# Batch 1 of an attention and MLP kernel: the last weight quarter issued later, behind a square on GpSimd; state products moved ahead of scores; groups that read that quarter moved behind the values

## The chip, the core and the metric

The kernel runs on one core of a Trainium2 chip. The core has five engines that run side by side and wait for each other through semaphores: TensorE (matmuls; PE in the profile, its weight loads PEld), VectorE (DVE), ScalarE (ACT), GpSimd (POOL) and SyncE (SP), which here only issues DMAs. Each engine works its own instructions strictly in the order of the program. Sixteen DMA engines move data between HBM and the on-chip memory SBUF; DMAs are issued from the queues of SP (loads, stores, transposes) and of POOL (weight loads that cast from float32 to float16 on the way). Matmul results stand in PSUM, which has eight banks, and an engine has to read a bank before another result may take its place.

The metric is the device time of one execution in microseconds. Before the change the median of 3 runs is 296.44 us (296.11 to 296.5).

## What is computed

Retention (attention without a softmax, with a decay by distance) of 8 batches, 8 heads, 576 positions and head size 64, and behind it an MLP on all 4608 tokens whose activation is x + sin²(αx)/α:

```python
scores = (1/8) * q @ k.T                       # per batch and head
ret    = scores * D                            # D[i, j] = gamma_h**(i - j) for i >= j, else 0
x      = (ret @ v)                             # heads side by side: 4608 x 512
h      = x @ w_in                              # 512 -> 2048
g      = h + sin(alpha * h)**2 / (alpha + 1e-9)
out    = g @ w_out                             # 2048 -> 512
```

## The kernel before

**Attention of a batch.** The first 512 positions of a batch are taken in two pieces (p = 0, 1) of 256 positions, each in two chunks of 128. For each piece `load` brings q, k and v from HBM (512 KB each, on SP's queue), `cast` turns them into float16 with the decay factors multiplied in, and q and k are transposed (for batch 1 on TensorE by `turn`, with `take` copying the result out of PSUM). Inside a chunk the retention is computed directly: `scores` (16 small matmuls for a half of the heads of a piece), `masked` (a VectorE multiplication with the mask), `values`. What lies in earlier chunks comes in through a state: `outer((p,))` computes the state products k-transposed times v of piece p (32 small matmuls of 64x64), `take_sum` copies them out, `more` adds the earlier chunks' sum (GpSimd), `to_state` makes the float16 state of it, and `add_states` multiplies it with q. `keep` copies the finished x of a piece out of PSUM. `values(p, True)`, which adds the second part, and `add_states` follow `values(p, False)`.

**MLP of a block** of 512 tokens. For each of 16 slices of the inner dimension (u or fc = 0 to 15) `project` multiplies x with w_in (4 matmuls of 512 columns), `sine` is ScalarE's sine, `square` its square (on ScalarE, VectorE or GpSimd, by the last argument A_, V or G_), and `product` on VectorE makes the slice of g, called gT, and with that releases the projection's bank. The second multiplication is done in groups: `gemm2(0, u, bank)` with u = 4c + part multiplies the 128 tokens of quarter c with the slices 4·part to 4·part + 3 of w_out, 4 matmuls of 512 columns, into the bank of quarter c; after the four parts `finish(0, c)` copies the bank out (ScalarE) and stores it (SP). So the groups 3, 7, 11 and 15 read the last quarter of w_out, which `load_w_out(3)` loads (one DMA on POOL's queue, a cast from float32 on the way).

**Order.** Everything up to batch 4 is written out by hand, instruction by instruction; each engine's order is the order of these lines. The code around the change finishes the MLP of block 0 while it does the attention of batch 1 and then begins the MLP of block 1 (`project(1, 7, ...)`, which needs both `keep` of batch 1). The buffers of the float32 loads (`raw0` to `raw5`) and of the squares (`ss0` to `ss3`) are reused in a fixed order, and banks are named by hand ("op", "h0" to "h2" single, "m0", "m1" double).

The steps of which the prediction speaks:

- L908 to L919: square 10 on GpSimd, the state of batch 0 (`to_state(3, G_)`), and the issue of the last quarter of w_out, all on POOL; L937 to L938, the load and GpSimd cast of the first v piece ("v0") of batch 1; L949 to L950 the same for its second k piece ("k1"); L957 to L958 the load of its second v piece ("v1") and its cast on ScalarE.
- L945 to L972: on TensorE the scores of piece 0, the state products of piece 0, groups 5 and 6, the transposition of k1, group 14, the scores of piece 1, group 15, the state products of piece 1 (`outer((1,), ...)`, which need the cast of v1), groups 7 and 0.
- L974 to L1013: the values and added states of both pieces, groups 1 and 2, and the two `keep`; L978 is VectorE's cast of q of batch 2.
- L1014 to L1024: projections 7 and 6, group 3, sines 7 and 6, square 6, `finish(0, 0)`, projection 13 into bank "h2", projection 8 into "op".

In the profile all projections bear the line L568, all groups L605, all casts of k and q L207, all copies on ScalarE L120, on VectorE or GpSimd L122; scores are L389, masks L401, state products L325, values L430, added states L451.

Of the kernel before, what the change touches and what calls it, by code (L numbers as in the profile page):

```python
# [36 lines left out]
def kernel(  # L37
# [68 lines left out]
    V, A_, G_ = nc.vector, nc.scalar, nc.gpsimd  # L106
# [5 lines left out]
    def load_w_out(g):  # L112
        nc.gpsimd.dma_start(w_out16[:, 4 * g : 4 * g + 4, :], w_out_r[:, g])
# [4 lines left out]
    def copy(eng, d_, s_):  # L118
        if eng is nc.scalar:
            eng.copy(d_, s_)  # L120
        else:
            eng.tensor_copy(d_, s_)  # L122
# [4 lines left out]
    def place(tag, shape, dtype):  # L127

        name = tag + next(slot_of[tag])
        if name not in places:  # L130
            places[name] = work.tile(shape, dtype, tag=name, bufs=1, name=name)
        return places[name]
# [14 lines left out]
    def load(b, nm, p):  # L147
        if p < 2 and b >= HALVED and nm != "q":
            t_ = place("raw", [P, H, 2 * D], F32)
            for g in range(2):  # L150
                for r in range(2):
                    s0 = 256 * p + 128 * g + 64 * r
                    nc.sync.dma_start(
                        t_[halves(g), :, r * D : r * D + D], src[nm][b, :, s0 : s0 + 64, :].rearrange("h i d -> i h d")
                    )
        elif p < 2:
            t_ = place("raw", [P, H, 2 * D], F32)
            nc.sync.dma_start(
                t_, src[nm][b, :, 256 * p : 256 * p + 256, :].rearrange("h (i r) d -> i h (r d)", r=2)
            )  # L160
        else:
            if b % 2 == 0:
                if b < 4:
                    raw[b, nm, 2] = work.tile([P, H, D], F32, tag="raws", bufs=3, name=nm + "s32")
                else:
                    raw[b, nm, 2] = ends_home(b, nm)
            t_ = raw[b - b % 2, nm, 2]
            nc.sync.dma_start(t_[halves(b % 2)], src[nm][b, :, 512:576, :].rearrange("h i d -> i h d"))
        raw[b, nm, p] = t_
# [77 lines left out]
    def take(b, nm, p, eng, ys=(0, 1)):  # L247
        d_ = new_T(b, nm, p).rearrange("p x n -> p (x n)")
        cols = slice(512 * ys[0], 512 * ys[-1] + 512)
        copy(eng, d_[:, cols], trs[b, nm, p][:, cols])  # L250
# [304 lines left out]
    def bank(tag):  # L555
        if tag[0] == "m":
            return psum.tile([P, 2, 512], F32, tag=tag, bufs=1, name="hps")[:, 0]
        return psum.tile([P, 512], F32, tag=tag, bufs=1, name="hps")

    def project(n, fc, tag, part=None):  # L560

        if n not in gT:
            gT[n] = work.tile([P, FC, 512], F16, tag="gT", bufs=2, name="gT")
        if (n, fc) not in hps_of:
            hps_of[n, fc] = [bank(tag), None]
        cols = PART[part]
        for a in range(KT):
            matmul(  # L568
                hps_of[n, fc][0][:, cols], w_in16[fc // 4][:, a, fc % 4 :: 4], xs[n][:, a, cols],
                start=(a == 0 and part != 1), stop=(a == KT - 1), skip_group_check=True,  # L570
            )

    def sine(n, fc):
        hps = hps_of[n, fc][0]
        s_t = place("s", [P, 512], F16)
        nc.scalar.activation(  # L576
            s_t, hps, mybir.ActivationFunctionType.Sin, bias=0.0, scale=alpha_t[:, fc : fc + 1],
        )
        hps_of[n, fc][1] = s_t

    def square(n, fc, eng):
        s_t = hps_of[n, fc][1]
        ss_t = place("ss", [P, 512], F16)
        if eng is nc.scalar:
            nc.scalar.activation(ss_t, s_t, mybir.ActivationFunctionType.Square)  # L585
        else:
            eng.tensor_tensor(ss_t, s_t, s_t, MULT)  # L587
        hps_of[n, fc][1] = ss_t

    def product(n, fc):  # L590
        hps, ss_t = hps_of.pop((n, fc))
        nc.vector.scalar_tensor_tensor(gT[n][:, fc, :], ss_t, inva[:, fc : fc + 1], hps, MULT, ADD)  # L592

    def finish(n, c, eng=None):
        osb = work.tile([P, 512], F32, tag="osb", bufs=4, name="osb")
        copy(eng or nc.scalar, osb, ops[n, c, 0])
        r0 = 576 * n + 128 * c
        nc.sync.dma_start(out[r0 : r0 + 128, :], osb)

    def gemm2(n, u, tag, cols=slice(0, 512)):  # L600
        c, part = divmod(u, 4)
        if (n, c, cols.start) not in ops:
            ops[n, c, cols.start] = psum.tile([P, 512], F32, tag=tag, bufs=1, name="ops")
        for fk in range(4 * part, 4 * part + 4):
            matmul(  # L605
                ops[n, c, cols.start][:, cols], gT[n][:, fk, c * P : (c + 1) * P], w_out16[:, fk, cols],
                start=(fk == 0), stop=(fk == FC - 1), skip_group_check=True,
            )
# [113 lines left out]
    at = [Attention(b) for b in range(B)]  # L722
# [13 lines left out]
    def wait_for_w_in(g):  # L736

        nc.sync.dma_start(gate, w_in16[g][:, 0, 0:64])
# [42 lines left out]
    with tc.manual_schedule():  # L781
# [134 lines left out]
        sine(0, 10)  # L916
        square(0, 10, G_)
        at[0].to_state(3, G_)
        load_w_out(3)  # L919
        wait_for_w_in(3)  # L920
        product(0, 5)
        project(0, 14, "h2")
# [3 lines left out]
        sine(0, 12)  # L926
        at[1].scores(0, 0, "m1")
        at[1].masked(0, 0)
        square(0, 12, A_)
        project(0, 13, "h0")  # L930
        sine(0, 13)
        square(0, 13, A_)
# [10 lines left out]
        product(0, 13)  # L943
        product(0, 12)
        at[1].scores(0, 1, "m0")  # L945
        at[1].outer((0,), "h0", "h1")
        at[1].take_sum(1, A_)
        gemm2(0, 5, "op")
        load(1, "k", 1)  # L949
        cast(1, "k", 1, G_)  # L950
        gemm2(0, 6, "op")
# [9 lines left out]
        take(1, "k", 1, V, (1,))  # L961
        take(1, "k", 1, V, (0,))
        gemm2(0, 14, "h2")
        at[1].scores(1, 1, "m0")
        at[1].masked(1, 1)
        at[1].scores(1, 0, "m1")
        at[1].masked(1, 0)
        gemm2(0, 15, "h2")
        at[1].outer((1,), "h0", "h1")
        at[1].take_sum(2, A_)  # L970
        at[1].more(2)
        gemm2(0, 7, "op")  # L972
        gemm2(0, 0, "h0")
        at[1].values(1, False, "m0")  # L974
        load(2, "q", 1)
        load(2, "k", 1)
# [26 lines left out]
        load(3, "v", 1)  # L1003
        load(4, "v", 0)
        load(3, "q", 1)
        finish(0, 1)
        at[1].to_state(2, A_)
        finish(0, 3)
        at[1].values(1, True)
        at[1].add_states(1)  # L1010
        gemm2(0, 1, "h0")
        gemm2(0, 2, "h0")
        at[1].keep(1, A_)  # L1013
        project(1, 7, "m1")  # L1014
        project(1, 6, "m0")
        gemm2(0, 3, "h0")
        sine(1, 7)
        sine(1, 6)
        square(1, 6, A_)
        finish(0, 0)  # L1020
        product(1, 6)
# [433 lines left out]
```

## Time and profile before

| | |
|---|---|
| median of 3 runs | 296.44 us (296.11 to 296.5) |
| the profiled execution | 298.54 us |
| its span, from the first to the last instruction | 296.8 us |
| TensorE busy | 284.6 us |
| VectorE busy | 227.5 us |
| ScalarE busy | 207.3 us |
| GpSimd busy | 136.0 us |
| mean granted clock of TensorE | 0.994 |

The profile is of one execution, with times in microseconds from its first instruction. A row of the timeline gives start, duration, engine, line, operation, what is written and read, and how many instructions were merged; in brackets stands how long the engine was idle before it and what ended that. Matmuls are pipelined: a row's duration runs over the start of the next, so distances are read from start to start. "PEclk" or "granted clock" is the share of full speed that TensorE's clock got. A "q" behind an engine's name (SPq, POOLq) is its sequencer, that is the issue of a DMA and not the transfer. In the rows of the DMA queues stand packets, megabytes, and the time that the packets took as a share of 16 engines' time; overlapping packets can make this more than 100%.

### The profile page before, as it was taken

The numbers are of one execution on the slowest core, as the hardware profiler recorded it, in microseconds if no ns is written. First come the engines' busy times: TensorE is split into PE (matmuls) and PEld (weight loads), VectorE is DVE, ScalarE is ACT, GpSimd is POOL, SyncE is SP. The second block draws the span as 40 slices with busy tenths as digits, with TensorE's granted clock in tenths as the row PEclk, the third lists the DMA queues.
The fourth block names the chain that finished last, engine by engine and source line by source line (L and its number), as shares of the span: only waits on it lengthen the run. The fifth ranks groups of instructions, "written<-read, shape, count | busy, mean of one in ns | idle before, by whom it ended". The sixth has DMA issues, their size and how long they took to land. (4 is left out here: it accounts for less than half of the span.)

```text
span 296.8 us, 8464 instructions
## 1 busy us (share of the span) xinstructions
PE 284.6 (96%) x3480; PEld 183.6 (62%) x3480; DVE 227.5 (77%) x336; ACT 207.3 (70%) x341; POOL 136.0 (46%) x151
## 2 busy tenths in 40 slices
PE   6789997999999999999999999999999999999994
PEld 4666544555554554455767766776667676777783
DVE  2597873897628979778977598759876987987884
ACT  2579924798776796788866996698669657865510
POOL 5684676448299687652197219901970000000000
PEclk9999997999999999999999999999999999999999
DMA  7999999999899698967876897789962102111213
GB/s 218 347 232 210 247 255 286 281 257 242 220 204 218 102 185 175 270 162 143 156 200 202 147 189 183 220 145 157 222 163 58 40 10 81 35 38 35 71 33 111
DMA packets 122918, 50.08 MB, mean 169 GB/s; under 512 B 79872, under 2 KB 120832, under 8 KB 122880
## 3 DMA queue, kind: packets, MB, share of 16 engines
q1 hardware_dynamic: 118928, 44.78, 62.7%
q0 software_dynamic: 2688, 4.19, 7.8%
q10 hardware_dynamic: 1264, 0.58, 0.8%
q8 instruction: 27, 0.44, 0.6%
q14 instruction: 11, 0.09, 0.1%
HBM read 36.75 MB, written 9.44 MB: 156 GB/s over the span
## 5 line engine op out<-in xcount | busy, mean ns | idle before, releaser
L592 DVE SCALAR_TENSOR_TENSOR gT<-ss,inva,hps 128x512 f16<-128x512 f16 x144 | 105.4, 744 | 29.2 <-ACT ss L585 25.3
L576 ACT ACTIVATE s<-hps,alpha_t 128x512 f16<-128x512 f32 x144 | 96.8, 682 | 44.3 <-PE hps L568 43.9
L568 PE MATMUL hps<-xT,w_in 128*128 128x512 f16 (+1 forms) x532 | 121.3, 372 | 0.7 <-DMA w_in<-in_moe_w_in_dram 0.3
L568 PEld LDWEIGHTS <-w_in 128*128 128x128 f16 x596 | 66.6, 114 | 50.7 <-issue 1.4
L585 ACT ACTIVATE ss<-s 128x512 f16<-128x512 f16 x107 | 67.3, 630 | 2.8
L605 PE MATMUL ops<-w_out,gT 128*128 128x512 f16 x192 | 47.6, 385 | 0.0
L671 PEld LDWEIGHTS <-gT 128*128 128x128 f16 x384 | 37.5, 98 | 8.3
L207 POOL TENSOR_TENSOR k<-raw,cn 128x1024 f16<-128x1024 f32 (+1 forms) x17 | 28.9, 1703 | 7.5 <-DMA raw<-in_k_dram 7.5
L671 PEld LDWEIGHTS <-S 128*128 128x128 f16 x288 | 27.7, 98 | 5.3
L605 PEld LDWEIGHTS <-gT 128*128 128x128 f16 x192 | 18.1, 99 | 20.8 <-issue 0.6
L363 POOL TENSOR_TENSOR s<-kvs,cn 128x256 f16<-128x256 f32 x17 | 10.4, 612 | 41.8 <-DVE S L652 25.4
L207 POOL TENSOR_TENSOR q<-raw,cn 128x1024 f16<-128x1024 f32 x13 | 24.6, 1903 | 4.5 <-DMA raw<-in_q_dram 4.3
L671 PE MATMUL hps<-T,gT 128*128 128x256 f16 x192 | 22.9, 273 | 0.0
L671 PE MATMUL hps<-w_out,gT 128*128 128x256 f16 x192 | 22.9, 273 | 0.0
L671 PE MATMUL hps<-w_out,S 128*128 128x256 f16 x192 | 22.8, 273 | 0.0
L401 DVE TENSOR_TENSOR ret<-sc,mask 128x1024 f16<-128x1024 f32 x16 | 19.2, 1219 | 1.6 <-PE sc L389 1.4
L371 POOL TENSOR_TENSOR kvs<-s,kvs 128x256 f32<-128x256 f32 x21 | 16.0, 762 | 5.5 <-ACT kvs L120 2.8
L120 ACT CAST xT<-o 128x1024 f16<-128x1024 f32 (+1 forms) x15 | 16.5, 1129 | 2.7 <-PE o L451 2.7
L587 DVE TENSOR_TENSOR ss<-s 128x512 f16<-128x512 f16 x29 | 14.3, 495 | 3.0 <-ACT s L576 2.8
L370 POOL TENSOR_TENSOR s<-kvs,cn 128x256 f32<-128x256 f32 x21 | 13.3, 635 | 6.4 <-ACT kvs L120 6.3
L717 DVE TENSOR_TENSOR osb<-hps,low 128x512 f32<-128x512 f32 x13 | 9.0, 692 | 9.2 <-PE hps L671 9.2
L652 DVE TENSOR_TENSOR S<-gT,S 128x1024 f16<-128x1024 f16 x24 | 15.5, 685 | 0.0
(83 smaller groups left out, 274.6 us busy)
## 6 DMA issues: line engine op xcount, KB each, us to landing
raw<-in_q_dram SPq DMA_DIRECT2D x16, 512.0 KB, 5.4
out_dram<-osb SPq DMA_DIRECT2D x32, 256.0 KB, 2.8
raw<-in_k_dram SPq DMA_DIRECT2D x8, 512.0 KB, 6.1
raw<-in_v_dram SPq DMA_DIRECT2D x8, 512.0 KB, 5.3
raw<-in_v_dram SPq DMA_DIRECT2D x32, 128.0 KB, 3.4
raw<-in_k_dram SPq DMA_DIRECT2D x32, 128.0 KB, 3.2
w_in<-in_moe_w_in_dram POOLq DMA_DIRECT2D x4, 512.0 KB, 11.8
w_out<-in_moe_w_out_dram POOLq DMA_DIRECT2D x4, 512.0 KB, 13.1
```

The source lines that it names most:

```text
L120: eng.copy(d_, s_)
L207: eng.tensor_tensor(dst[:, a0:a1].rearrange("p a r t d -> p t (a r) d"), t_.rearrange("p (t a) x -> p t a x", t=2)[:, :, a0:a1].rearrange( ...
L371: nc.gpsimd.tensor_tensor(self.kvs[:, c], s32, self.kvs[:, c], ADD)
L401: nc.vector.tensor_tensor(ret.rearrange("p t (z x) -> p (t z) x", z=2)[:, :, 0:n], sc.rearrange("p t (z x) -> p (t z) x", z=2)[:, :, 0:n], ...
L568: matmul(hps_of[n, fc][0][:, cols], w_in16[fc // 4][:, a, fc % 4 :: 4], xs[n][:, a, cols], start=(a == 0 and part != 1), stop=(a == KT - 1 ...
L576: nc.scalar.activation(s_t, hps, mybir.ActivationFunctionType.Sin, bias=0.0, scale=alpha_t[:, fc : fc + 1],)
L585: nc.scalar.activation(ss_t, s_t, mybir.ActivationFunctionType.Square)
L587: eng.tensor_tensor(ss_t, s_t, s_t, MULT)
L592: nc.vector.scalar_tensor_tensor(gT[n][:, fc, :], ss_t, inva[:, fc : fc + 1], hps, MULT, ADD)
L605: matmul(ops[n, c, cols.start][:, cols], gT[n][:, fk, c * P : (c + 1) * P], w_out16[:, fk, cols], start=(fk == 0), stop=(fk == FC - 1), sk ...
L652: return eng.tensor_tensor(out_, x, y, op)
L671: matmul(acc[:, 256 * j : 256 * j + 256], lhs[:, x, 128 * j : 128 * j + 128], rhs[:, x], start=(tag is not None and j == js[0] and p == 0 ...
```

## The change

The issue of the last quarter of w_out moves back on POOL, behind square 12, which moves from ScalarE to GpSimd. Group 5 comes ahead of the state products of piece 0. The state products of piece 1 with their copy and sum come ahead of the scores of piece 1. Groups 1 and 2 come ahead of the values; groups 15 and 7, which read the last quarter, come behind values and added states and behind both `keep`, with `finish(0, 1)` right after them. `finish(0, 3)` comes behind the sines 7 and 6. Nothing is added and nothing left out but the engine of one square.

```diff
         square(0, 10, G_)
         at[0].to_state(3, G_)
-        load_w_out(3)
         wait_for_w_in(3)
...
         at[1].masked(0, 0)
-        square(0, 12, A_)
+        square(0, 12, G_)
+        load_w_out(3)
         project(0, 13, "h0")
...
         at[1].scores(0, 1, "m0")
+        gemm2(0, 5, "op")
         at[1].outer((0,), "h0", "h1")
         at[1].take_sum(1, A_)
-        gemm2(0, 5, "op")
         load(1, "k", 1)
...
         gemm2(0, 14, "h2")
+        at[1].outer((1,), "h0", "h1")
+        at[1].take_sum(2, A_)
+        at[1].more(2)
         at[1].scores(1, 1, "m0")
         at[1].masked(1, 1)
         at[1].scores(1, 0, "m1")
         at[1].masked(1, 0)
-        gemm2(0, 15, "h2")
-        at[1].outer((1,), "h0", "h1")
-        at[1].take_sum(2, A_)
-        at[1].more(2)
-        gemm2(0, 7, "op")
         gemm2(0, 0, "h0")
+        gemm2(0, 1, "h0")
+        gemm2(0, 2, "h0")
         at[1].values(1, False, "m0")
...
-        finish(0, 1)
         at[1].to_state(2, A_)
-        finish(0, 3)
         at[1].values(1, True)
         at[1].add_states(1)
-        gemm2(0, 1, "h0")
-        gemm2(0, 2, "h0")
         at[1].keep(1, A_)
+        gemm2(0, 7, "op")
+        gemm2(0, 15, "h2")
+        finish(0, 1)
         project(1, 7, "m1")
         project(1, 6, "m0")
         gemm2(0, 3, "h0")
         sine(1, 7)
         sine(1, 6)
+        finish(0, 3)
         square(1, 6, A_)
```

## The prediction

> **What bounds the kernel now.** First the page: its span and its busy shares.
>
> ```profile
> span 296.8 us, 8464 instructions
> ```
>
> ```profile
> PE 284.6 (96%) x3480; PEld 183.6 (62%) x3480; DVE 227.5 (77%) x336; ACT 207.3 (70%) x341; POOL 136.0 (46%) x151
> ```
>
> PE (TensorE) is the bound, so a saving is a stretch in which PE stands or runs slowly. Second, what PE waited for from 52 us to the end, behind the edited code (in total, times, longest).
>
> ```profile
> PE hps L568 <- DVE gT L592: 0.3, 1, 0.3
> ```
>
> It is 0.3 us in all: whatever PE gains or loses in the edited code arrives at the end nearly whole. Third, the edited code itself, PE and ScalarE in order of time (start, duration, idle time before it and its releaser).
>
> ```profile
> 42.85 0.64 PE L389 MATMUL sc<-qT,kT 64*64 64x128 f16 x32
> 43.43 1.04 PE L605 MATMUL ops<-w_out,gT 128*128 128x512 f16 x4
> 46.43 0.45 PE L325 MATMUL kv<-v,k 64*64 64x64 f16 x32 [1.96 <-ACT v L120]
> 46.80 2.79 PE L605 MATMUL ops<-w_out,gT 128*128 128x512 f16 x8
> 49.52 1.75 PE L430 MATMUL o<-ret,v 64*64 64x128 f16 x48
> ```
>
> ```profile
> 51.76 1.47 PE L605 MATMUL ops<-w_out,gT 128*128 128x512 f16 x6
> ```
>
> ```profile
> 45.33 1.04 ACT L120 CAST v<-raw 128x1024 f16<-128x1024 f32 x1 [5.36 <-DMA raw<-in_v_dram]
> ```
>
> The load of batch 1's second v piece ("v1" below) lands late, ScalarE's cast of it starts at 45.33 after 5.36 us of waiting, and PE's state products (L325) wait 1.96 us for the cast. Fourth, busy time by stretches (PE, PEld, DVE, ACT, POOL, then granted clock, DMA share, GB/s).
>
> ```profile
> 44.25:47.67 3.42, 1.46 (x37) 0.84 (x37) 2.36 (x3) 1.42 (x2) 0.58 (x2) 1.00 0.90 259
> 47.67:51.08 3.41, 3.31 (x53) 1.67 (x55) 0.30 (x1) 2.12 (x6) 3.41 (x3) 0.50 1.05 311
> ```
>
> After a stretch in which PE was busy 1.46 of 3.42 us, the granted clock is 0.50 for 3.41 us: the wait is paid twice. What the clock costs is read against the same steps of batch 2 and a later row of groups, both at full clock.
>
> ```profile
> 75.73 1.15 PE L430 MATMUL o<-ret,v 64*64 64x128 f16 x48
> ```
>
> ```profile
> 77.27 0.78 PE L325 MATMUL kv<-v,k 64*64 64x64 f16 x64
> 77.98 5.35 PE L605 MATMUL ops<-w_out,gT 128*128 128x512 f16 x24
> 83.17 0.59 PE L568 MATMUL hps<-xT,w_in 128*128 128x512 f16 x2
> ```
>
> From start to start, 24 matmuls of 512 columns take 83.17 - 77.98 = 5.19 us, 0.216 each; values and added states take 77.27 - 75.73 = 1.54. In the slow stretch, eight matmuls took 49.52 - 46.80 = 2.72 in place of 1.73, and values and states 51.76 - 49.52 = 2.24 in place of 1.54: 0.99 + 0.70 = 1.69 us for the clock, beside 1.96 of standing.
>
> Fifth, why v1 is late: the issues of SP and POOL, and what the DMA queues moved (packets, MB, share of 16 engines; q1 carries SP's loads, q0 POOL's), with their landings: first from 33 to 37.3 us, then the single microsecond from 36, then that from 39.
>
> ```profile
> 32.70 0.72 SPq L158 DMA_DIRECT2D raw<-in_k_dram  x1
> 33.51 2.91 SPq L158 DMA_DIRECT2D raw<-in_v_dram  x1
> ```
>
> ```profile
> 35.10 0.60 POOL L113 DMA_DIRECT2D w_out<-in_moe_w_out_dram  x1
> 37.98 1.03 POOL L122 CAST v<-raw 128x1024 f16<-128x1024 f32 x1 [2.29 <-DMA raw<-in_v_dram]
> 39.49 1.90 POOL L207 TENSOR_TENSOR k<-raw,cn 128x1024 f16<-128x1024 f32 x1 [0.47 <-DMA raw<-in_k_dram]
> ```
>
> ```profile
> q1 hardware_dynamic: 1862, 0.89, 70.5%
> ```
>
> ```profile
> raw<-in_k_dram SPq DMA_DIRECT2D x1, 512.0 KB, 6.7
> ```
>
> ```profile
> w_out<-in_moe_w_out_dram POOLq DMA_DIRECT2D x1, 512.0 KB, 7.9
> ```
>
> ```profile
> q1 hardware_dynamic: 690, 0.35, 115.0%
> q0 software_dynamic: 1, 0.00, 0.1%
> ```
>
> ```profile
> q0 software_dynamic: 48, 0.17, 87.5%
> q1 hardware_dynamic: 35, 0.02, 6.4%
> ```
>
> A load is 512 KB, 0.52 MB. SP's order is v0, k1, v1. By 37.3 q1 had moved 0.89 MB, less than v0 and k1 together (1.05); k1 lands at 32.70 + 6.7 = 39.4. Then the w_out quarter, issued at 35.10 while SP was still handing over v1 (33.51 to 36.42), holds the engines: in the microsecond from 39, q0 moves 0.17 MB and q1 0.02. v1 stands behind the quarter.
>
> **The change, part by part.** *Quarter and square.* Square 12 on GpSimd needs sine 12 of ScalarE; its duration is that of GpSimd's square just before.
>
> ```profile
> 34.61 0.67 ACT L576 ACTIVATE s<-hps,alpha_t 128x512 f16<-128x512 f32 x1
> ```
>
> ```profile
> 33.54 1.04 POOL L587 TENSOR_TENSOR ss<-s 128x512 f16<-128x512 f16 x1 [0.57 <-ACT s L576]
> ```
>
> Sine 12 ends at 35.28, the square near 36.35, and the quarter is issued there, 1.24 later than now. Its one DMA passes only this square on POOL's queue; nothing on SP's queue moves. The square itself costs nothing: POOL stands from 35.70 to 37.98, and product 12 is the last of its group. Without that cover it would push the v0 cast by 1.04. SP has handed v1 over (36.42) before the quarter's first bytes can move; today none had moved by 37, some 2 us behind the issue. In which order an engine then serves the two, no row shows. One bound: v1 goes ahead whole and lands 0.52/0.35 = 1.5 us behind k1, at 40.9. The other: the quarter still goes first, 45.33 as now. I take the first: today k1, handed over before the quarter was ready, ran through on the slowest engine too (39.4), and v1 now stands to the quarter as k1 did.
>
> [...]
>
> *State products ahead of the scores.* With v1 at 40.9, ScalarE's cast (1.04) ends near 42.0. PE comes to the products at 42.85, where the scores start today (both need k1's transposed copy taken). No wait. From there: products 46.80 - 46.43 = 0.37, scores 43.43 - 42.85 = 0.58, groups 0, 1 and 2 12 x 0.216 = 2.59, values and states 1.54, groups 7 and 15 1.73. Projection 7 starts at 49.66 instead of 53.50:
>
> ```profile
> 53.50 1.89 PE L568 MATMUL hps<-xT,w_in 128*128 128x512 f16 x8
> ```
>
> ```profile
> 56.09 7.17 PE L568 MATMUL hps<-xT,w_in 128*128 128x512 f16 x36
> ```
>
> **-3.84 us.** Beside it lie VectorE's two masks and q's cast, then the copy of x:
>
> ```profile
> 43.32 2.36 DVE L401 TENSOR_TENSOR ret<-sc,mask 128x1024 f16<-128x1024 f32 x2 [0.47 <-PE sc L389]
> 46.74 1.23 DVE L207 TENSOR_TENSOR q<-raw,cn 128x1024 f16<-128x1024 f32 x1 [1.06 <-DMA raw<-in_q_dram]
> ```
>
> ```profile
> 51.44 1.31 DVE L122 CAST xT<-o 128x1024 f16<-128x1024 f32 x1 [3.47 <-PE o L451]
> ```
>
> The masks end near 46.1 and values start at 46.4; q's cast ends at 47.97 if its load lands as now, the copy of x at 49.28. That is just in time; each microsecond by which q is later costs one.
>
> *Group 5 ahead of the first products* delays their sums by 4 x 0.216 = 0.86. GpSimd, which uses them next, is in k1's cast until 41.39, and the sums would be there near 40.8: nothing, and 0.86 on the way to batch 1's states without that cover.
>
> *Groups 7 and 15 behind the values.* The quarter lands at 43.0 today (35.10 + 7.9); they run near 48, so its lateness has some 4 us of cover, beyond which each microsecond costs one. Their copies (finish 1 and 3) move too. Projection 13 takes the bank of group 15, whose copy now stands behind sine 6 on ScalarE:
>
> ```profile
> 55.42 0.69 ACT L576 ACTIVATE s<-hps,alpha_t 128x512 f16<-128x512 f32 x1 [0.18 <-PE hps L568]
> ```
>
> ```profile
> 56.68 0.57 ACT L120 COPY osb<-ops 128x512 f32<-128x512 f32 x1
> ```
>
> Sine 6 ends 2.61 behind the start of projection 7, the copy 0.57 later, so projection 13, now 2.59 behind, starts 0.6 later: **+0.6**, a new wait of PE. Behind that copy are queued square 6, copy 0 and sine 13, and PE waits for these no longer than now. The two stores keep their place on SP, behind loads.
>
> *What is late next:* batch 2's state products, which need GpSimd's v casts.
>
> ```profile
> 58.06 2.31 POOL L122 CAST v<-raw 128x1024 f16<-128x1024 f32 x2 [3.27 <-PE hps L568]
> ```
>
> ```profile
> 63.18 0.71 PE L325 MATMUL kv<-v,k 64*64 64x64 f16 x64
> ```
>
> The casts end at 60.37; the products would start at 63.18 - 3.24 = 59.94. If the casts stay where they are, that costs 0.43; if they move with PE, as their releaser says, 0. I take **+0.24**, about the middle. The sum: -3.84 + 0.6 + 0.24 = **-3.0 us**. The profiled execution took 298.54, of which 1.74 lie around its span; it would take 295.5. Against the median of the runs, 296.44, that is **293.4**.
>
> **The rivals.** *The quarter still first: slower.* If on even one of the 16 DMA engines the quarter goes ahead as now, v1's cast starts at 45.33 again, and PE stands at the products from 42.85 to 46.43, 3.58 us in place of 1.96, since scores and group 15 no longer lie in front of them. Beside the forecast that is +3.58, and the clock falls as it does today, +1.69: **+2.3 us, 298.7**; +0.6, 297.0, if it holds. With the clock's loss it is slower from 3.0 - 1.69 = 1.31 behind 42.85 on, which is a landing of v1 at about 43.1. For it: 1.24 us is less than a load's 1.5, and engines differ (at 0.35 MB/us the mean one has v0 and k1 by 37.8, the last at 39.4), so the last comes to its choice when the quarter is ready. Against it: v1's hand-over comes first. That the change doesn't do what it says is this case.
>
> *By turns.* An engine done with k1 serves the quarter, then v1: from 39.4, the quarter's 0.52 MB at the 0.19 MB/us of the microsecond from 39 take 2.8, v1 1.5. v1 lands at 43.7, the products start near 44.8, 1.95 behind the forecast: -1.05, or +0.64 with the clock's loss; in the middle **-0.2 us, 296.2**. For it: v1 got its turn today only behind the quarter. Against it: the quarter would have had to break into k1 today. [...]
>
> [...]
>
> **How the numbers follow.** Forecast 0.57, its own range 292.6 (no new wait at all) to 294.7 (1.3 of the gain eaten by q's cast or the v casts). By turns 0.18, the quarter first 0.25. The low end is 292.6; the high end reaches into the slower rival, between its 297.0 and 298.7, to 298.0, which leaves some 0.15 above and 0.05 below. 0.2%, 0.6 us, is about what a measurement of this kernel can tell from no change. Faster: 0.56 + 0.06 = 0.62; same: 0.01 + 0.08 + 0.01 = 0.10; slower: 0.04 + 0.24 = 0.28.
>
> **What would show it.** Right: the quarter's issue near 36.3; v1's cast starting near 41 and no PE wait at L325; granted clock 1.00 from 47 to 51; projection 7 near 49.7; a PE wait of 0.6 before projection 13. Wrong: v1's cast still behind 43, a longer wait at L325 and a stretch at 0.50; or q's cast or GpSimd's v casts as new releasers of PE.

## The result and the profile after

Median of the changed kernel 296.15 us (295.2 to 297.04, 14 runs), of the kernel before 296.27 (295.03 to 297.0, 14 runs): a ratio of 1.0, with a 95% interval of 0.9984 to 1.0015. That is no change that can be measured, where the forecast was a gain, to 293.4. The time lies in the range given and close to the 296.2 of the middle rival, but by luck: what that rival says did not happen, as the experiments show. The profiled execution of the changed kernel took 296.01.

Its page first, span and busy shares:

```profile
span 294.3 us, 8464 instructions
...
PE 282.9 (96%) x3480; PEld 182.5 (62%) x3480; DVE 227.3 (77%) x336; ACT 206.5 (70%) x340; POOL 136.6 (46%) x152
```

The span is 2.5 us shorter than that of the profiled execution before. Then PE in order of time at the edited place (start, duration, idle time before it and its releaser):

```profile
42.74 0.49 PE L325 MATMUL kv<-v,k 64*64 64x64 f16 x32
43.05 0.64 PE L389 MATMUL sc<-qT,kT 64*64 64x128 f16 x32
...
49.77 1.89 PE L568 MATMUL hps<-xT,w_in 128*128 128x512 f16 x8
...
52.91 1.02 PE L568 MATMUL hps<-xT,w_in 128*128 128x512 f16 x4 [0.39 <-ACT osb L120]
```

GpSimd's issue of the quarter and ScalarE's cast of v1, the same view:

```profile
36.36 0.60 POOL L113 DMA_DIRECT2D w_out<-in_moe_w_out_dram  x1
```

```profile
40.89 1.05 ACT L120 CAST v<-raw 128x1024 f16<-128x1024 f32 x1
```

Then the two stretches whose clock the prediction quotes (PE, PEld, DVE, ACT, POOL busy, then granted clock, DMA share, GB/s):

```profile
44.25:47.67 3.42, 3.32 (x83) 1.81 (x84) 2.74 (x3) 1.06 (x4) 1.67 (x3) 1.00 1.13 338
47.67:51.08 3.41, 3.41 (x47) 1.78 (x36) 3.38 (x6) 2.01 (x3) 2.95 (x2) 1.00 1.00 299
```

Each thing that the change was to do is there: the quarter goes out at 36.36, v1's cast starts 4.4 us earlier, there is no wait at the state products (L325), the clock is full in both stretches, and projection 7 starts at 49.77 instead of 53.50. Yet the time of the kernel is what it was. What PE waits for from 52 us to the end (in total, times, longest):

```profile
PE hps L568 <- DVE gT L592: 0.9, 2, 0.7
PE hps L568 <- ACT osb L120: 0.4, 1, 0.4
```

That is 1.3 us instead of 0.3, too little to eat 3.7. So either the gain is lost in a way the waits don't show, or the other executions of the kernel before never had the loss.

### The profile page after: what moved, and what is told of

The parts are those of the page before. It is cut to its first block, busy times and chain, and to the rows that moved or that the text cites. A ratio compares the mean times of both kernels' runs of the same rounds, so it can differ in the third digit from the quotient of the medians.

```text
span 294.3 us, 8464 instructions
## 1 busy us (share of the span) xinstructions
PE 282.9 (96%) x3480; PEld 182.5 (62%) x3480; DVE 227.3 (77%) x336; ACT 206.5 (70%) x340; POOL 136.6 (46%) x152
## 5 line engine op out<-in xcount | busy, mean ns | idle before, releaser
L592 DVE SCALAR_TENSOR_TENSOR gT<-ss,inva,hps 128x512 f16<-128x512 f16 x144 | 105.3, 743 | 30.2 <-ACT ss L585 26.1
L585 ACT ACTIVATE ss<-s 128x512 f16<-128x512 f16 x106 | 66.6, 631 | 2.8
L605 PE MATMUL ops<-w_out,gT 128*128 128x512 f16 x192 | 46.8, 379 | 0.0
L207 POOL TENSOR_TENSOR k<-raw,cn 128x1024 f16<-128x1024 f32 (+1 forms) x17 | 29.7, 1750 | 9.0 <-DMA raw<-in_k_dram 8.2
L401 DVE TENSOR_TENSOR ret<-sc,mask 128x1024 f16<-128x1024 f32 x16 | 19.1, 1217 | 2.1 <-PE sc L389 2.0
L587 DVE TENSOR_TENSOR ss<-s 128x512 f16<-128x512 f16 x29 | 13.5, 469 | 3.3 <-ACT s L576 3.2
```

Source lines behind the costliest of these rows:

```text
L207: eng.tensor_tensor(dst[:, a0:a1].rearrange("p a r t d -> p t (a r) d"), t_.rearrange("p (t a) x -> p t a x", t=2)[:, :, a0:a1].rearrange( ...
L401: nc.vector.tensor_tensor(ret.rearrange("p t (z x) -> p (t z) x", z=2)[:, :, 0:n], sc.rearrange("p t (z x) -> p (t z) x", z=2)[:, :, 0:n], ...
L605: matmul(ops[n, c, cols.start][:, cols], gT[n][:, fk, c * P : (c + 1) * P], w_out16[:, fk, cols], start=(fk == 0), stop=(fk == FC - 1), sk ...
```

## The experiments

The theory tested first: the profiled execution of before was untypical (298.54, where the 14 runs of before end at 297.0). Its rival: each execution has the wait and the slow stretch, and the gain is given back later.

**Both kernels again, unchanged.**

> The kernel of before, unchanged. Theory A, the execution that the prediction was read from was not a typical one: v1's landing and the clock's stretches move from one execution to the next, so this profile has a span of 293.3 to 295.3 us (14 timed runs had 295.0 to 297.0, some 1.7 around the span), and either the cast of v1 starts before 44 us or no stretch near 47 to 51 us has the clock 0.50. Theory B, every execution has the wait of 2 us and the half clock, and what the change gains there is lost behind it: cast of v1 at 45.3, clock 0.50 for 3.4 us, span 296.8. Ratio to itself 1.000 in both.

> The changed kernel, unchanged. Theory A: as in its first profile, v1's cast near 41, no wait at the state products, projection 7 at 49.8, span 293.5 to 295.3, ratio 1.000 within 0.3%. Theory B: the same start, but in some executions a later loss that its first profile did not show: projection 7 at 49.8 and a span above 295.3, or a stretch of half clock behind 60 us.

Before: 296.14 (295.0 to 297.22, 12 runs), ratio to the shared runs of before 0.9998, interval 0.9979 to 1.0017. Its profile, ScalarE's cast, then PE:

```profile
43.45 1.05 ACT L120 CAST v<-raw 128x1024 f16<-128x1024 f32 x1 [3.49 <-DMA raw<-in_v_dram]
```

```profile
42.82 0.64 PE L389 MATMUL sc<-qT,kT 64*64 64x128 f16 x32
43.39 1.04 PE L605 MATMUL ops<-w_out,gT 128*128 128x512 f16 x4
44.55 0.45 PE L325 MATMUL kv<-v,k 64*64 64x64 f16 x32
44.93 1.90 PE L605 MATMUL ops<-w_out,gT 128*128 128x512 f16 x8
46.76 1.15 PE L430 MATMUL o<-ret,v 64*64 64x128 f16 x48
...
48.69 1.90 PE L605 MATMUL ops<-w_out,gT 128*128 128x512 f16 x8
50.43 1.89 PE L568 MATMUL hps<-xT,w_in 128*128 128x512 f16 x8
```

Two stretches of 3.41 us from there, and what PE waits for from 52 us on:

```profile
43.53:46.94 3.41, 3.29 (x56) 1.51 (x58) 3.25 (x3) 1.93 (x3) 2.41 (x3) 1.00 1.00 298
46.94:50.36 3.42, 3.33 (x96) 2.08 (x89) 2.29 (x6) 2.73 (x6) 3.42 (x3) 1.00 1.12 334
```

```profile
PE hps L568 <- DVE gT L592: 0.6, 1, 0.6
PE hps L568 <- DVE ret L401: 0.3, 1, 0.3
```

It is the same program, and the cast of v1 starts 1.88 us earlier. It ends at 44.50, and PE begins the products at 44.55: scores and group 15, which stand in front of them, cover the late load almost exactly. The profile lists no wait there and no slow stretch; the span is 294.4. The changed kernel again took 296.49, ratio 1.0015 (0.9991 to 1.004), and its profile is like the first one: cast of v1 at 40.80, no wait at the products, projection 7 at 49.77.

**A third profile of before.**

> The kernel before once more, for its profile. If the first profile was untypical, v1's cast starts near 43.4 again, PE does not wait at the state products behind the scores, and no stretch has a granted clock of 0.50; span near 294.4. If the first was typical, the wait of about 2 us and the 0.50 are back.

It took 296.3, its span is 294.6. ScalarE's cast, PE at the products and at projection 7, and what PE waits for:

```profile
43.31 1.05 ACT L120 CAST v<-raw 128x1024 f16<-128x1024 f32 x1 [3.50 <-DMA raw<-in_v_dram]
```

```profile
44.41 0.45 PE L325 MATMUL kv<-v,k 64*64 64x64 f16 x32
...
50.28 1.89 PE L568 MATMUL hps<-xT,w_in 128*128 128x512 f16 x8
```

```profile
PE hps L568 <- DVE ret L401: 0.6, 1, 0.6
PE hps L568 <- DVE gT L592: 0.4, 1, 0.4
```

Two of three profiles of before have no wait at this place, and they are the two whose times lie at the median. For the timed runs without a profile, the mean granted clock is on record. A stretch of 3.41 us at 0.50 loses 1.7 us of some 296 and so leaves a mean of 0.994 at most, which is what the first profile has. Of the 68 runs of before that were made beside the experiments, 34 have a mean of 0.997 or more and so hold no such stretch. Their median is 296.43, that of all 68 is 296.46: the usual time of before is a time without the slow stretch.

**The two parts of the change alone.** First the quarter and its square, in the order of before:

```diff
-        load_w_out(3)
...
-        square(0, 12, A_)
+        square(0, 12, G_)
+        load_w_out(3)
```

> Only the quarter and square 12 move; TensorE's order stays that of before. Theory A: v1's cast near 41 as in the changed kernel, so the state products (behind the scores and group 15) find it done, no wait, no 0.50, and also no wait before projection 13: as fast as the changed kernel or up to 0.4 us faster, ratio 0.997 to 1.000. Theory B: the wait vanishes, ratio 0.988 or less unless something later takes it.

It took 296.28 (295.04 to 298.01, 12 runs), ratio 0.9999 (0.9978 to 1.0019). The profiled execution was one of the longer ones, 297.07, with a span of 295.4. The same views of it (cast, PE, waits of PE from 52 us on):

```profile
40.76 1.05 ACT L120 CAST v<-raw 128x1024 f16<-128x1024 f32 x1 [0.87 <-DMA raw<-in_v_dram]
```

```profile
44.40 0.45 PE L325 MATMUL kv<-v,k 64*64 64x64 f16 x32
...
49.99 1.89 PE L568 MATMUL hps<-xT,w_in 128*128 128x512 f16 x8
```

```profile
PE hps L568 <- DVE gT L592: 0.8, 1, 0.8
PE kv L325 <- POOL v L122: 0.5, 1, 0.5
PE hps L568 <- DVE ret L401: 0.3, 1, 0.3
PE sc L389 <- DMA qT<-q: 0.3, 1, 0.3
```

The later quarter brings v1 forward by 2.7 us, and nobody was waiting for it. Then the order alone, with the quarter where it was (the changed kernel but for these lines):

```diff
+        load_w_out(3)
...
-        square(0, 12, G_)
-        load_w_out(3)
+        square(0, 12, A_)
```

> Only the order moves; the quarter is issued where it was, square 12 stays on ScalarE. Theory A: when v1 lands late TensorE stands at the state products for as long as the landing is behind 41.8 us, without the scores and group 15 in front: up to 3.6 us of wait, slower by 0.3 to 2.3 us, ratio 1.001 to 1.008, with a spread from execution to execution. Theory B: always 3.6 us of wait and half clock, slower by 2.3 us, ratio 1.008.

It took 297.96 (296.32 to 299.44, 10 runs), ratio 1.0063 (1.004 to 1.0087): slower than before. The span is 296.3. The same views:

```profile
43.42 1.04 ACT L120 CAST v<-raw 128x1024 f16<-128x1024 f32 x1 [2.53 <-DMA raw<-in_v_dram]
```

```profile
44.51 0.45 PE L325 MATMUL kv<-v,k 64*64 64x64 f16 x32 [1.67 <-ACT v L120]
...
51.50 1.89 PE L568 MATMUL hps<-xT,w_in 128*128 128x512 f16 x8
```

```profile
PE hps L568 <- DVE gT L592: 1.0, 2, 0.6
PE hps L568 <- ACT osb L120: 0.4, 1, 0.4
```

PE comes to the products 1.67 us before v1 is cast, since the order took its cover away, and the wait reaches the end: 0.63% is 1.9 us. So the new order needs the later quarter, and the later quarter has a use only in the new order; together they come out even.

**v1 handed over later.** In both kernels SP hands over batch 2's q piece ahead of v1 (with their buffers kept):

```diff
+        load(2, "q", 1)
         load(1, "v", 1)
...
-        load(2, "q", 1)
```

> The kernel before, with batch 1's second v piece (v1) issued on SP one load later: behind the q piece of batch 2 that came next. Its v1 cast should start about one load (1.5 us) behind the 43.45 of the typical execution, near 45, as in the first profile of before (45.33). If the stall there was real and reaches the end, PE waits 1.5 to 2 us at the state products (L325) and the time is 1.5 to 2 us (0.5 to 0.7%) above before; with a granted clock of 0.50 in the stretch behind it, some 1.7 more, 3.2 to 3.7 us (1.1 to 1.25%). If lost time at this place is made up later, the time stays within 0.2% although the wait shows.

> The changed kernel with the same delay of v1: v1 is now handed over while the w_out quarter, issued near 36.4, becomes ready. If the quarter then goes first on some engine, v1's cast starts near 45 and PE, which comes to the products at 42.7 with nothing in front of them, waits some 3.3 us: 1.1% slower, 1.7% with a fall of the clock. If the quarter waits for what was handed over about when it was, v1 lands only one load later than in the changed kernel, its cast starts near 42.4 and PE waits about 0.7 us: 0.2% slower. In the first case the change is no protection against a late v1 but makes it dearer than in the kernel before; in the second it is one.

The kernel before with it took 298.07 (296.13 to 299.23, 10 runs), ratio 1.0041 (1.0014 to 1.0067). Cast, products, and two stretches of 3.41 us, laid out in such steps from where the granted clock changes in that profile:

```profile
45.79 1.04 ACT L120 CAST v<-raw 128x1024 f16<-128x1024 f32 x1 [5.84 <-DMA raw<-in_v_dram]
```

```profile
46.88 0.45 PE L325 MATMUL kv<-v,k 64*64 64x64 f16 x32 [2.48 <-ACT v L120]
```

```profile
42.54:45.95 3.41, 1.86 (x38) 0.89 (x37) 2.94 (x4) 0.16 (x1) 1.92 (x4) 1.00 0.94 272
45.95:49.36 3.41, 2.48 (x60) 1.30 (x63) 0.79 (x1) 2.28 (x6) 1.47 (x2) 1.00 1.08 314
```

The wait is longer than in the first profile of before (2.48 against 1.96), and the clock stays at 1.00. The 0.41% are 1.2 us, somewhat under the 1.5 to 2 expected for a wait without a fall of the clock (the interval allows 0.4 to 2.0); a loss at this place does reach the end. The changed kernel with it took 300.45 (300.18 to 301.68, 4 runs), ratio 1.015 (1.0105 to 1.0194), which is 4.5 us. The hand-overs of GpSimd and SP, the cast, PE, and the stretches:

```profile
36.29 0.60 POOL L113 DMA_DIRECT2D w_out<-in_moe_w_out_dram  x1
```

```profile
36.47 1.40 SPq L158 DMA_DIRECT2D raw<-in_v_dram  x1
```

```profile
44.96 1.04 ACT L120 CAST v<-raw 128x1024 f16<-128x1024 f32 x1 [4.03 <-DMA raw<-in_v_dram]
```

```profile
46.06 0.45 PE L325 MATMUL kv<-v,k 64*64 64x64 f16 x32 [3.17 <-ACT v L120]
```

```profile
43.84:47.25 3.41, 1.17 (x66) 0.98 (x66) 0.47 (x1) 1.42 (x2) 0.89 (x3) 1.00 1.15 343
47.25:50.66 3.41, 3.41 (x10) 1.22 (x9) 3.41 (x3) 1.06 (x4) 3.41 (x3) 0.50 1.03 293
```

The first of the two expected cases: v1, handed over from 36.47 on, now stands behind the quarter issued at 36.29, and PE pays the wait and the clock. This is the slower rival of the prediction (the quarter still first, 2.3 us), here brought about by one load more ahead of v1 on SP's queue; it costs more than those 2.3 us, since the base holds no wait and no slow stretch to set against it. A late v1 costs the changed kernel more than the kernel before.

**The new wait taken away.** In the changed kernel, the copy of group 15 right behind that of group 7:

```diff
         finish(0, 1)
+        finish(0, 3)
         project(1, 7, "m1")
...
         sine(1, 6)
-        finish(0, 3)
```

> The changed kernel with the copy of group 15 (finish of columns 3) issued right behind that of group 7, ahead of the sines 7 and 6 on ScalarE, where ScalarE stands for 0.92 us. The wait of 0.39 before projection 13 goes. If PE's time at this place reaches the end, 0.4 us (0.13%) less than the changed kernel, which five rounds hardly tell from nothing; a larger gain would mean the copy holds up more than that wait.

It took 296.27 (295.07 to 297.69, 12 runs), ratio 0.9993 (0.9972 to 1.0014). PE in order of time, and its waits from 52 us on:

```profile
49.76 1.89 PE L568 MATMUL hps<-xT,w_in 128*128 128x512 f16 x8
...
52.35 6.00 PE L568 MATMUL hps<-xT,w_in 128*128 128x512 f16 x31
```

```profile
PE sc L389 <- DMA qT<-q: 1.1, 1, 1.1
PE hps L568 <- DVE gT L592: 0.8, 1, 0.8
```

Projection 13 starts 0.56 earlier, at 52.35, without a wait; but the span is 294.6, no shorter than the 294.3 of the changed kernel. PE waits for a transposed q and for VectorE later, 1.9 us in all. No version here beats both kernels by what can be measured.

## Why the prediction was wrong

**The step that failed is the base.** The prediction took the wait of 1.96 and the stretch at 0.50 from one profiled execution as what the kernel before does, and then subtracted their worth from the median of the runs ("Against the median of the runs, 296.44, that is 293.4"). But that median does not contain them. In the two other profiles v1 is cast from 43.31 or 43.45, not 45.33, and the profile lists no wait of PE for it. The sign was on the table: the profiled execution took 298.54, 2.1 us more than the median of three runs that lay within 0.4 us of each other, and its span exceeds those of the other two by 2.2 and 2.4. The prediction named the gap and carried it along as an offset instead of asking whether the stall was the gap. Worked on the rows of the repeated profile, its own sum gives almost nothing: projection 7 moves from 50.43 to 49.77, 0.66 us, against its +0.6 and +0.24.

**Measured against its own execution, most of the working held.**
- The quarter's issue was forecast for 36.34 and came at 36.36; products at 42.85 without a wait, 42.74 measured; projection 7 at 49.66, 49.77 measured: -3.73 for -3.84.
- The choice that v1 goes ahead whole (40.9) held: its cast starts between 40.76 and 40.89 in the four profiles that have the later quarter and v1 handed over as before. In the changed order it follows right on a copy of ScalarE, so v1 may have been there a little earlier; in the profile of the quarter alone the DMA releases it, at 40.76. The middle rival, by turns, with 43.7, did not come about. What the later quarter rests on is shown by the late pair: with v1 handed over from 36.47 on, it loses.
- Masks, q's cast and the copy of x came in time, as said.
- The wait for the copy of group 15: +0.6 forecast, 0.39 measured. GpSimd's v casts start at 56.58 instead of 58.06 and end before PE comes to the products at 59.92, so the +0.24 was 0.
- The clock's price of 1.69 was too high for the kernel before. From the products to projection 7 the profiled before took 53.50 - 46.43 = 7.07, the repeated one at full clock 50.43 - 44.55 = 5.88: 1.19. Values and added states of batch 1 take 48.69 - 46.76 = 1.93, not the 1.54 borrowed from batch 2. With the 1.88 by which the products came earlier, that makes the 3.07 between the two executions at projection 7. In the changed kernel the price is nearer the forecast: with v1 late it takes 54.73 - 46.06 = 8.67 from products to projection 7, at full clock 49.77 - 42.74 = 7.03, so 1.64.

**"Whatever PE gains or loses in the edited code arrives at the end nearly whole" was too strong for gains.** It rested on 0.3 us of waits behind 52 us in one profile. From the start of projection 7 to the end of the span, with the waits behind 52 us, in all ten profiles:

| kernel | projection 7 | rest of span | waits behind 52 | rest without them |
|---|---|---|---|---|
| changed, v1 late | 54.73 | 244.1 | 0.9 | 243.2 |
| before, first profile | 53.50 | 243.3 | 0.3 | 243.0 |
| before, v1 late | 52.47 | 244.1 | 1.1 | 243.0 |
| order alone | 51.50 | 244.8 | 1.4 | 243.4 |
| before, second | 50.43 | 244.0 | 0.9 | 243.1 |
| before, third | 50.28 | 244.3 | 1.0 | 243.3 |
| quarter alone | 49.99 | 245.4 | 1.9 | 243.5 |
| changed | 49.77 | 244.5 | 1.3 | 243.2 |
| changed, second | 49.77 | 244.6 | 1.4 | 243.2 |
| changed, copies early | 49.76 | 244.8 | 1.9 | 242.9 |

The last column hardly moves, so what decides is how long PE stands behind 52 us: for VectorE's products (L592), masks (L401), a copy, a cast or a transposed q. The 0.3 is the smallest of the ten; the others have 0.9 to 1.9, the most where PE comes earliest, though not in step with it. Of the 3.7 us gained at projection 7 on the first profile of before, 2.5 arrive; of the 0.66 gained on the second, 0.1. Losses go through: the order alone is 1.73 behind the changed kernel at projection 7 and 2.0 at the end, the changed kernel with v1 late 4.96 and 4.5.

What stays open is why v1 landed 1.9 us later in that one execution (the quarter in front of it landed later too: 35.10 + 7.9 = 43.0, against 34.90 + 7.1 = 42.0 and 34.94 + 6.9 = 41.8), and in how many of the timed runs it does. Single long runs occur in both kernels: one of the 23 runs of before beside the late pair took 300.19, and two of the 12 of the repeated changed kernel 298.46 and 299.36. None of them has a profile. Nor was it tried what the clock costs when the wait falls elsewhere in a step of 3.41 us (see the last section) in the same kernel.

## What to carry to other kernels

When the profiled execution lies outside the spread of the timed runs, the stall that one is about to price may be the very reason it does; a second profile of the unchanged kernel settles that before any sum is made. And ask of a wait not how long it is but how much cover stands in front of it: here scores and one group just hid the load, so bringing the load forward alone gained nothing, and taking the cover away alone cost 0.6%. And the waits behind an edit, read from one profile, do not say what an engine will meet there when it comes earlier: here they were 0.3 us in the profile of the forecast and 0.9 to 1.9 in the nine others.

## What the runs showed of the hardware

In these profiles the granted clock does not follow from the length of a gap. Waits of 1.96 and 3.17 us were followed by 3.41 us at 0.50; one of 2.48 and one of 1.67 were not. What orders these four is the busy time of PE within steps of 3.41 us, the length of the two stretches at 0.50, laid out by the author in each profile from where its clock changes: 1.46 of 3.42 and 1.17 of 3.41 were followed by 0.50, 1.86 of 3.41 by 1.00, and so was the emptiest step around the edit in the profile of the order alone:

```profile
40.77:44.18 3.41, 2.07 (x15) 0.96 (x14) 1.55 (x4) 0.88 (x2) 3.25 (x6) 1.00 1.11 328
```

In the late kernel before, the gap of 2.48 was split between two steps, and PE was busy 1.86 and 2.48 us in them. So a wait of about 2 us cost 1.2 us more in one execution of this kernel (7.07 from the products to projection 7, in place of 5.88) and a longer one nothing more in another (52.47 - 46.88 = 5.59). What differs between these two profiles is where the wait fell in steps so laid out. Of the steps around the edit, PE was busy 0.43 and 0.34 of those followed by 0.50, and 0.55 or more of those followed by 1.00; none lay between.

In the profiles quoted here, which of the two DMA queues went first turned on which hand-over ended first. With the quarter issued at 35.10 (to 35.70), while SP was still handing v1 over (to 36.42), v1's cast starts at 45.33 (in the other two profiles of before at 43.45 and 43.31). With the quarter issued at 36.36, when SP had just handed v1 over (33.26 to 36.17), it starts at 40.89. In the changed kernel with v1 late the quarter's issue at 36.29 (to 36.89) stands just ahead of v1's hand-over from 36.47 on (to 37.87), and the cast starts at 44.96. In the profile of the changed kernel as it stands the quarter moved its first bytes only in the microsecond from 39, where SP's queue had moved loads alone before (first the microsecond from 38, then that from 39):

```profile
q1 hardware_dynamic: 619, 0.32, 109.8%
```

```profile
q0 software_dynamic: 34, 0.14, 68.7%
q1 hardware_dynamic: 316, 0.16, 51.9%
```

Here v1, when it was first, was not slowed by as much as the rival by turns reckoned (its cast at 40.89, against a landing at 43.7), but the quarter moved nothing until SP's queue had moved 1.42 MB from 33 to 39 us, where v0, k1 and v1 are 1.57, so a taking of turns was hardly put to the test.
